# Windowed attention scores as column tiles of 32 queries: eight small matmuls of 160 keys in place of two of 256

## The chip, the cores and the metric

The kernel runs on one core of a Trainium2 chip. The metric is the device time of one execution in microseconds (us); lower is better. Several executions of the unchanged kernel are timed, and one more is taken by the hardware profiler.

## What is computed

Four sequences of 576 tokens, eight heads of 64. A query sees the 128 keys that end with its own, under a bias that falls linearly with the distance. The result feeds a mixture of four experts over all 2304 tokens, all in f32:

```python
scores = scale * np.matmul(q, k.transpose(0, 1, 3, 2))
rel = pos[:, None] - pos[None, :]
bias = slopes[:, None, None] * (-np.abs(rel).astype(np.float32))[None, :, :]
mask = (rel >= 0) & (rel < window)                      # window = 128
scores = np.where(mask, scores + bias[None], -1000000000.0)
attn = np.exp(scores - np.max(scores, axis=-1, keepdims=True))
attn = attn / (np.sum(attn, axis=-1, keepdims=True) + 1e-09)
out = np.matmul(attn, v)
...
for e in range(E):                                      # 4 experts, 512 -> 1024 -> 512
    h = np.maximum(x @ w1[e], 0.0)
    out += p[:, e:e + 1] * (h @ w2[e])
```

## The kernel before, in words

**Order.** Every piece of work is first noted as an operation of a planner (`Plan.op`): which engine may do it, a cost per engine, a due time, what it reads and writes and the buffers it needs. `Plan.order` then lays all of them out greedily, by engine, and the instructions are emitted in that order. [...] The costs are numbers in the file (`PLAIN * mm(n)` for scores, `VALUED * mm(n)` for values, and so on); an operation may also ask for a margin (`late`), which for the values operation is `LATE_V = 1.903` us. `FILL = 80` matmuls of a tile of ones into an idle bank (`multiplied`, L1827) have the latest due time of all: the planner sets one wherever it has nothing else for PE, and PE executes it there.

**Work.** The tokens are cut into seven blocks (`BLOCKS`: three of 256, four of 384) and the heads into four pairs, so there are 28 segments (block, pair). The four segments of block 0 are "plain" and done by an older recipe at the start. The other 24 segments hold 64 units, a unit being 128 queries of one pair of heads. Attention runs from the start to about 375 us, laid between the matmuls of the experts (`hidden` L1340, `output` L1760, `opening` L1248, which is the first block's first product with the expert weights; later `sevenfold` L1397 and `pair` L1656, both after or beside attention). The experts need the attention output of a block (`xh`, `xl`) before they can start on it.

**A unit** (function `unit`, not plain):

1. Scores (`scores`, L650): for each of the two heads one f32 matmul of 128 queries by up to 256 keys, the 128 of the tile before and the tile's own. Head 0 sits on partitions 0 to 63, head 1 on 64 to 127, so the two are row tiles of the array. Up to two units share one planner operation and one pair of PSUM banks.
2. Fold (L714): DVE copies, under a mask (`after`), the keys of the tile before over those own keys that the query must not see; a query then has its 128 keys in 128 columns, in rotated order.
3. DVE adds the bias and finds the maximum (L725), ACT takes exponents (L743), DVE or ACT divides (L774, L781).
4. Turn: DVE transposes blocks of 32x32 (L825), one DMA writes the unit to a DRAM buffer (`tr`), four read it back turned (`s<-tr`).
5. POOL splits it with `affine_select` into the keys of the tile itself and of the tile before (L857), into `pb`.

At a segment's last unit, values (`values`, L904) multiplies with v: 128x64 column tiles, one per head. `gathered` splits the result into `xh` and `xl`.

In the profile an f32 matmul is two records (two passes); the expert matmuls are one.

Of the kernel before, what the change touches and what calls it, by code (L numbers as in the profile page):

```python
# [16 lines left out]
NEG = -1.0e30  # L17
# [197 lines left out]
VALUED = 2.95  # L215
SWITCH = 0.09
# [67 lines left out]
def attention_moe(  # L284
# [41 lines left out]
    places("s", 3, [P, 2, 2 * P], F32)  # L326
    halves_ = [t[:, i] for t in plan.places["s"] for i in range(2)]
    plan.places["sv"], plan.places["tu"] = halves_[:NSV], halves_[NSV:]
    places("t", 6, [P, 6], F32)
    turns, again = [sb.tile([P, 6, 2 * P], F32, tag=f"pb{i}", name=f"pb{i}") for i in range(2)], {}  # L330
# [28 lines left out]
    places("tr", TURNS, [P, 2 * P], F32, dr)  # L359
# [14 lines left out]
    after = sb.tile([P, 2, P], F32, tag="after", name="after")  # L374
# [155 lines left out]
    for nb, (s0, n) in enumerate(BLOCKS):  # L530
        for hp in range(NPAIR):
            g = Rec()
            g.nb, g.hp, g.plain, g.units = nb, hp, nb == 0, []
            g.s0, g.n, g.k0 = s0, n, s0 - before(s0 // P)
            g.v0 = g.k0 // P
            g.kn, g.vn = s0 + n - g.k0, (s0 + n) // P - g.v0
            for i in range(n // P):
# [4 lines left out]
                u.q0, u.k0, u.vt = i * P, (u.tile * P - u.pk) - g.k0, u.tile - g.v0  # L542
# [70 lines left out]

    def unit(u):
# [10 lines left out]
        if g.plain:  # L625
            scored = [Buf("b"), Buf("b")]
            sh = lambda h: scored[h][:, :n]
        else:
            at = u.q0 // P
            if at % 2 == 0:  # L630
                g.scored = [Buf("b"), Buf("b")]
            scored, sc0 = g.scored, 2 * P * (at % 2)
            sh = lambda h: scored[h][:, sc0 : sc0 + n]
# [6 lines left out]
        if not g.plain:  # L640
            at = u.q0 // P
            mine = g.units[at : at + 2] if at % 2 == 0 else []

        def scores(e):
            for x in mine:
                c0 = 0 if g.plain else 2 * P * (x.q0 // P % 2)
                for h in range(2):
                    r = (lo64, hi64)[h]
                    qv, kv = (g.q, g.k) if g.plain else (g.q[:, 0], g.k[:, 0])
                    nc.tensor.matmul(  # L650
                        scored[h][:, c0 : c0 + x.pk + P],
                        qv[r, g.qo + x.q0 : g.qo + x.q0 + P],
                        kv[r, x.k0 : x.k0 + x.pk + P],
                        start=True,
                        stop=True,
                        skip_group_check=not g.plain,
                    )

        qk = [(g.shared[0], g.hp % 2, h) for h in range(2)] if g.plain else [g.q, g.k]
        if mine:  # L660
            plan.op(
                {PE: sum(PLAIN * mm(x.pk + P) for x in mine)},
# [5 lines left out]
                sum(PLAIN * mmc(x.pk + P) for x in mine),  # L668
# [6 lines left out]
        if g.plain:  # L675

# [4 lines left out]
            if pk:  # L681
                plan.op({POOL: 0.45}, seen(lambda: b2()[:, :, :P], bv, True), d - 1, [bkey], [(bb, 0)], port=(POOL,))
            else:
                plan.op({POOL: 0.45}, seen(lambda: b2()[:, :, P:], bv, False), d - 1, [bkey], [(bb, 1)], port=(POOL,))
            bv, bkey = (lambda: b2()[:, :, o:]), [(bb, 0), (bb, 1)][not pk :]
        elif edge or pk < P:
            bb = Buf("x")
            b2 = lambda: bb[:, : 2 * P].rearrange("p (h n) -> p h n", h=2)
            if edge:
                plan.op({POOL: 0.45}, lambda e: nc.gpsimd.tensor_copy(b2()[:edge], bias[:edge, hs, :]), d - 1, [bkey, "scores"], [(bb, 0)], port=(POOL,))  # L690
                plan.op({POOL: 0.2}, lambda e: nc.gpsimd.memset(b2()[edge:, :, :edge], NEG), d - 1, ["scores"], [(bb, 1)], port=())
                plan.op(
                    {POOL: 0.3},
                    seen(lambda: b2()[edge:, :, edge:], lambda: bias[edge:, hs, edge:], False),
                    d - 1,
                    [bkey, "scores"],
                    [(bb, 2)],
                    port=(POOL,),
                )
            else:  # L700
# [179 lines left out]
        if u.first:  # L880
            g.started, g.jobs = [False, False], []
            if not g.plain:
                g.av = Buf("b")
# [1147 lines left out]
```

## Time and profile before

| | |
|---|---|
| Median of 3 runs | 850.93 us (850.92 to 851.1) |
| The profiled execution's own time | 850.55 us |
| Its span, first to last instruction | 848.8 us |
| Granted TensorE clock, mean over the span | 1.00 |
| PE busy / DVE / ACT / POOL | 844.5 / 662.7 / 393.3 / 346.3 us |

Busy times count overlapping instructions once. [...]

### The profile page before, as it was taken

What the parts mean: (1) busy time and instruction counts of PE and PEld (TensorE: products, weight loads), DVE (VectorE), ACT (ScalarE), POOL (GpSimd) and SP (SyncE); (2) the same over time, 40 slices, a digit from 0 to 9 for tenths busy, and PEclk for the clock granted to TensorE, in tenths of its full rate; (3) what the DMA queues carried; (4) which work ended last, traced back from release to release, by engine and by line L of the source; (5) the groups of instructions that cost most, each with busy time, mean ns of one, the idle gap of its engine ahead of it and who ended that gap; (6) DMA issues with size and microseconds to landing.
All of it is one profiled execution on the core that took longest, in us unless ns stands there. A gap on an engine that the chain in (4) does not pass through costs nothing.

```text
span 848.8 us, 15203 instructions
## 1 busy us (share of the span) xinstructions
PE 844.5 (99%) x5050; PEld 748.3 (88%) x5050; DVE 662.7 (78%) x1621; ACT 393.3 (46%) x1019; POOL 346.3 (41%) x550
## 2 busy tenths in 40 slices
PE   9999999999999999999999999999999999999998
PEld 6888788777777778889898898998999999999998
DVE  7998767677866687748887777887798888788777
ACT  7754424354433355414553433442455544654552
POOL 2422422141332435226752326133656464454542
DMA  7877755466756467532787565744566346535602
GB/s 240 255 238 232 226 154 170 134 175 180 225 165 175 124 196 231 171 97 84 274 317 270 211 224 186 273 179 156 169 216 220 116 137 199 155 131 162 224 2 75
DMA packets 92464, 156.37 MB, mean 184 GB/s; under 512 B 42849, under 2 KB 63073, under 8 KB 88673
## 3 DMA queue, kind: packets, MB, share of 16 engines
q1 hardware_dynamic: 86528, 125.84, 45.6%
q0 software_dynamic: 5632, 29.36, 11.0%
q8 instruction: 40, 0.66, 0.3%
q14 instruction: 40, 0.32, 0.1%
q10 hardware_dynamic: 224, 0.20, 0.1%
HBM read 111.32 MB, written 44.04 MB: 183 GB/s over the span
## 4 chain that ended last, share of the span: by engine, by line
PE 98%; DVE 1%; issue 0%; ACT 0%; ACTq 0%
PE b L1760 32%; PE b L1397 25%; PE b L1340 18%; PE b L1656 13%; PE b L904 4%; PE b L650 4%; PE b L1827 1%; PE b L1248 1%; PE b L801 0%; DVE w1r L1182 0%; DVE xl L421 0%; DVE acc L725 0%; DVE b L1426 0%; DVE w1r L1570 0%; DVE q L1570 0%
## 5 line engine op out<-in xcount | busy, mean ns | idle before, releaser
L1760 PE MATMUL b<-w2h,halves 128*128 128x512 f32 x612 | 208.0, 394 | 0.0
L1340 PE MATMUL b<-xh,w 128*128 128x512 f32 (+2 forms) x576 | 153.2, 341 | 0.0
L1760 PEld LDWEIGHTS b<-w2h,halves 128*128 128x128 f32 x612 | 114.9, 188 | 26.2 <-issue 3.7
L1778 DVE SCALAR_TENSOR_TENSOR acc<-b,prob,acc 128x512 f32<-128x512 f32 x136 | 101.5, 746 | 32.3 <-PE b L1760 31.3
L1760 PE MATMUL b<-w2l,halves 128*128 128x512 f32 x306 | 120.1, 392 | 0.0
L857 POOL TENSOR_SCALAR_AFFINE_SELECT pb<-s 128x256 f32<-128x256 f32 x120 | 53.8, 473 | 153.5 <-DMA s<-tr 38.4
L1340 PEld LDWEIGHTS b<-xh,w 128*128 128x128 f32 x576 | 101.9, 189 | 13.6 <-issue 1.2
L1340 PE MATMUL b<-xl,w 128*128 128x512 f32 (+2 forms) x288 | 97.6, 339 | 0.0
L1297 ACT ACTIVATE halves<-b 128x256 fp32r<-128x256 f32 (+2 forms) x76 | 36.9, 488 | 94.4 <-PE b L1340 93.9
L421 POOL TENSOR_TENSOR w<-w1r,w 128x256 fp32r<-128x256 f32 x66 | 50.0, 779 | 73.0 <-DVE w L421 32.8
L1682 DVE SCALAR_TENSOR_TENSOR acc<-b,prob,acc 128x256 f32<-128x256 f32 x156 | 67.4, 476 | 12.2 <-PE b L1656 11.0
L1304 DVE SCALAR_TENSOR_TENSOR halves<-b,halves 128x256 fp32r<-128x256 f32 (+2 forms) x76 | 41.9, 553 | 44.6 <-ACT halves L1297 44.2
L743 ACT ACTIVATE s<-s,t 128x128 f32<-128x128 f32 x128 | 50.5, 395 | 49.8 <-DVE t L725 49.5
L1410 ACT ACTIVATE s<-b 128x384 f32<-128x384 f32 x87 | 42.6, 490 | 65.7 <-PE b L1397 65.3
L1397 PE MATMUL b<-xh,w 128*128 128x384 f32 x232 | 68.9, 337 | 0.0
L421 POOL TENSOR_TENSOR w2l<-w2r,w2h 128x256 fp32r<-128x256 f32 x52 | 39.5, 779 | 70.5 <-DVE w2l L421 23.0
L1760 PEld LDWEIGHTS b<-w2l,halves 128*128 128x128 f32 x306 | 57.5, 188 | 9.0
L401 ACT ACTIVATE w2h<-w2r 128x512 fp32r<-128x512 f32 x79 | 48.5, 625 | 24.4 <-PE b L1760 16.8
L1340 PEld LDWEIGHTS b<-xl,w 128*128 128x128 f32 x288 | 54.4, 189 | 6.1
L421 DVE TENSOR_TENSOR w2l<-w2r,w2h 128x512 fp32r<-128x512 f32 x76 | 54.9, 746 | 1.4 <-ACT w2h L401 1.2
L1397 PEld LDWEIGHTS b<-xh,w 128*128 128x128 f32 x232 | 42.9, 188 | 0.6
L1426 DVE TENSOR_TENSOR b<-b,s 128x384 f32<-128x384 f32 x58 | 32.6, 562 | 13.4 <-PE b L1397 9.1
(230 smaller groups left out, 2068.8 us busy)
## 6 DMA issues: line engine op xcount, KB each, us to landing
w2r<-in_w SPq DMA_DIRECT2D x59, 512.0 KB, 4.6
w1r<-in_w SPq DMA_DIRECT2D x43, 512.0 KB, 4.8
w<-parked POOLq DMA_DIRECT2D x16, 1024.0 KB, 5.2
parked<-w SPq DMA_DIRECT2D x13, 1024.0 KB, 4.9
tr<-s SPq DMA_DIRECT2D x64, 128.0 KB, 2.6
s<-tr SPq DMA_DIRECT2D x256, 32.0 KB, 2.5
vs<-parked POOLq DMA_DIRECT2D x8, 768.0 KB, 5.1
pt<-parked POOLq DMA_DIRECT2D x8, 768.0 KB, 4.6
```

Source lines behind the costliest of these rows:

```text
L401: return nc.scalar.activation(o(), i(), AF.Copy)
L421: by[e].tensor_tensor(out=x, in0=y, in1=f(z), op=ALU.subtract) for x, y, z in pieces(e, n, o(), a(), b())
L743: return lambda e: nc.scalar.activation(sv()[:, h, -m:], sv()[:, h, -m:], AF.Exp, bias=t[:, h : h + 1], scale=-1.0, accum_out=t[:, 2 + h : ...
L857: return lambda e: nc.gpsimd.affine_select(out=spread(2 * i + own), in_=wb.place, pattern=steps, base=0, channel_multiplier=-sign, compare ...
L1304: lambda e: nc.vector.scalar_tensor_tensor(out=lo[:, :n], in0=src(), scalar=0.0, in1=f(h[:, :n]), op0=ALU.max, op1=ALU.subtract,),
L1340: nc.tensor.matmul(bk[:, :n], a[0][:, kt, fs], b[:, kt, cols], start=kt == 0 and i == 0, stop=kt == KT - 1 and i == 2,)
L1397: nc.tensor.matmul(bank[:, :n], x(k), y(k), start=new and k == 0 and i == 0, stop=k == 1 and i == 2, skip_group_check=True,)
L1410: {ACT: act(n)}, lambda e: nc.scalar.activation(pv(p), bank[:, :n], AF.Copy), at[0] - URGENT, [bank], [p]
L1656: nc.tensor.matmul(bank[bk][part]()[:, cs], a()[:, ns], b()[:, fi, :], start=new and i != 1 and fi == 0 and j == 0, stop=fi == 1 and j == ...
L1682: nc.vector.scalar_tensor_tensor(out=ac[:, ds], in0=bank[bk][part]()[:, cs], scalar=prob[:, nt, e_ : e_ + 1], in1=ac[:, ds], op0=ALU.mult, ...
L1760: nc.tensor.matmul(bk[:, cs], a[:, ns], b[1][:, fi, cs], start=half != 1 and fi == 0 and j == 0, stop=half != 0 and fi == 1 and j == 2, sk ...
L1778: nc.vector.scalar_tensor_tensor(out=o, in0=i_, scalar=p, in1=o, op0=ALU.mult, op1=ALU.add)
```

## The change

Scores of a unit become eight matmuls: four column tiles of 32 queries (`FAST`), for each of two heads, each by the 160 keys (`WIDE`) that those 32 queries can see between them. All units of a segment, two or three, are one planner operation in one pair of banks. The order of the 128 keys left after the fold is now the same in each block of 32 queries, so the fold touches 32 columns a unit, and is done once a segment and head. The bias is rotated to match: its first 32 rows are loaded four times, and POOL makes the other heads of it; the plain segments keep the old bias in a `pb` buffer (`level`). Biases of tiles at a sequence's border are put together from more, smaller POOL pieces. A segment's weights (two or three units) go to DRAM in one write and come back in seven reads, straight into `pb`; POOL then makes the two parts with one select each for the whole segment. Units without a tile before them are no longer treated apart: they read the tile before and get a bias that hides it.

```diff
+TILED = 0.03
+SIDES = 1.1
+FAST = 32
+WIDE = 160
...
-    places("s", 3, [P, 2, 2 * P], F32)
...
+    st = sb.tile([P, 6, 2 * P], F32, tag="st", name="st")
+    plan.places["s"] = [st[:, 2 * i : 2 * i + 2] for i in range(3)]
+    plan.places["sv"], plan.places["tu"] = [st[:, i] for i in range(NSV)], [st[:, NSV:].rearrange("p i n -> p (i n)")]
...
+    def turned_over(g, wb, d, nu):
+        tr = Buf("tr")
+        m, w = 64 * nu, 2 * P * nu
+        flat_ = lambda: tr[:, :w]
+        load(lambda: flat_(), lambda: wb[:, :w], 512 * w, d + 0.8, [(wb, i) for i in range(nu)], [tr])
...
+        for kb in range(4):
+            for j0, j1 in ((0, kb + 1), (kb + 1, 4)):
+                if j0 < j1:
+                    g.rows.append((kb, j0))
+                    load(
...
+                        128 * m * (j1 - j0),
+                        d + 0.85,
+                        [tr],
+                        [(g.pt, (kb, j0))],
+                    )
...
+        plan.op({POOL: SIDES * nu / 3}, lambda e: side(e, False), d + 0.95, rows, [(g.pt, "earlier")])
+        plan.op({POOL: SIDES * nu / 3}, lambda e: side(e, True), d + 1.0, [], rows)
...
-            mine = g.units[at : at + 2] if at % 2 == 0 else []
+            mine = g.units if u.first else []
...
-                for h in range(2):
-                    r = (lo64, hi64)[h]
-                    qv, kv = (g.q, g.k) if g.plain else (g.q[:, 0], g.k[:, 0])
-                    nc.tensor.matmul(
-                        scored[h][:, c0 : c0 + x.pk + P],
-                        qv[r, g.qo + x.q0 : g.qo + x.q0 + P],
-                        kv[r, x.k0 : x.k0 + x.pk + P],
...
+                c0 = WIDE * (x.q0 // P)
+                qv, kv = (g.q[:, 0], g.k[:, 0])
+                for j in range(0, P, FAST):
+                    for h in range(2):
+                        r = (lo64, hi64)[h]
+                        nc.tensor.matmul(
+                            scored[h][j : j + FAST, c0 : c0 + WIDE],
+                            qv[r, g.qo + x.q0 + j : g.qo + x.q0 + j + FAST],
+                            kv[r, x.k0 + j : x.k0 + j + WIDE],
...
-                {PE: sum(PLAIN * mm(x.pk + P) for x in mine)},
+                {PE: sum(PLAIN * mm(x.pk + P) if g.plain else TILED + WIDE / 600 for x in mine)},
...
-        if fold and pk:
+        if fold and u.first:
+            nu = len(g.units)
             for h in range(2):
                 plan.op(
-                    {DVE: 0.07 + pk / 960},
+                    {DVE: 0.075 + nu * FAST / 960},
...
-                if pk:
-                for own in (0, 1):
-                    plan.op({POOL: 0.42}, side(own), d + 0.95 + 0.2 * own, raws_, [(g.pt, 2 * i + own)])
...
+            if u.last:
+                turned_over(g, wb, d, nu)
...
-    load(lambda: bias[:, 0, :], lambda: bfd[:, 0, :], 65536, -38, [], ["rel"], ACT)
+    level = Buf("pb")
+    load(lambda: level[:, :P], lambda: bfd[:, 0, :], 65536, -38, [], [(level, 0)], ACT)
+    for j in range(4):
+        load(lambda j=j: bias[32 * j : 32 * j + 32, 0, :], lambda: bfd[:32, 0, :], 16384, 0.1 * j, [], [("rel", j)])
...
+        plan.op({POOL: 0.8 if hp else 0.4}, rescaled(hp), 1 + hp, [("rel", j) for j in range(4)], [("bias", hp)])
```

The planner's table decides where everything lands, so three places of the order are shown. The first is on PE, in the first blocks, where a segment's scores follow the values of an earlier one (`b` is a PSUM bank, `k` and `q` the operands). Before, the pair of heads of each unit is one row each:

```order
716 L904 MATMUL b_115<-pb_85,v_67 64x128 x2
717 L904 MATMUL b_115<-pb_85,v_67 64x256 x4
718 L904 MATMUL b_115<-pb_85,v_67 64x128 x2
719 L650 MATMUL b_116<-k_66,q_64 128x256
720 L650 MATMUL b_118<-k_66,q_64 128x256
721 L650 MATMUL b_119<-k_65,q_63 128x256
722 L650 MATMUL b_121<-k_65,q_63 128x256
```

Of the changed kernel, half a unit stands here; a unit has eight such rows, one bank per head in turn, and the units of a segment follow each other without a break:

```order
158 L708 MATMUL b_113<-k_66,q_64 32x160
159 L708 MATMUL b_117<-k_66,q_64 32x160
160 L708 MATMUL b_113<-k_66,q_64 32x160
161 L708 MATMUL b_117<-k_66,q_64 32x160
```

Over the whole listing the 64 units are 128 score matmuls in 26 unbroken runs before, and 512 in 22 runs now; the values are the same rows as before.

The second place is PE's opening: `b<-xh,w` (L1248, now L1277) is the first product with expert weights, `b<-acc,v` (L904, now L933) the values of a plain segment, `b<-ident,acc` (L801, now L873) transposes of one. Before, the product begins between the plain segments:

```order
134 L904 MATMUL b_115<-acc_109,v_68 64x128
135 L1248 MATMUL b_117<-xh_89,w_97 128x256
136 L1248 MATMUL b_117<-xl_91,w_97 128x256
137 L1248 MATMUL b_117<-xh_89,w_97 128x256
138 L801 MATMUL b_118<-ident,acc_105 128x128 x2
139 L1248 MATMUL b_117<-xh_89,w_97 128x256
```

Now it begins behind the last plain segment's values, with filling matmuls on ones (L1869) ahead of them:

```order
191 L1869 LDWEIGHTS ones
192 L1869 MATMUL b_112<-ones 128x256
193 L933 MATMUL b_114<-acc_108,v_68 64x256
194 L933 MATMUL b_114<-acc_102,v_68 64x256
195 L933 MATMUL b_114<-acc_108,v_68 64x128
196 L933 MATMUL b_114<-acc_102,v_68 64x128
197 L1277 MATMUL b_119<-xh_87,w_95 128x256
```

Of the 80 fillings, 49 stand up to the opening's end before and 62 now; 18 and 14 stand later but ahead of PE's last product, 13 and 4 behind it.

The third place is SP's queue, where the weights are turned. Before, each unit has a write and four reads:

```order
101 L394 DMA tr_128<-s_78 128x256
102 L394 DMA s_78<-tr_127 32x4x64 x4
103 L394 DMA s_78<-tr_128 32x4x64 x4
104 L394 DMA tr_129<-s_77 128x256
```

Now a segment (here three units) has one write and seven reads:

```order
143 L399 DMA tr_121<-st 128x768
144 L399 DMA w2r_93<-in_w 128x1024
145 L399 DMA pb_83<-tr_121 32x192
146 L399 DMA pb_83<-tr_121 32x3x192
147 L399 DMA pb_83<-tr_121 32x2x192 x2
148 L399 DMA pb_83<-tr_121 32x3x192
149 L399 DMA pb_83<-tr_121 32x192
150 L399 DMA pb_83<-tr_121 32x4x192
```

## Rows read from the trace of the kernel before

**Rows 1.** The page: busy time by engine, and the chain that ended last.
```profile
PE 844.5 (99%) x5050; PEld 748.3 (88%) x5050; DVE 662.7 (78%) x1621; ACT 393.3 (46%) x1019; POOL 346.3 (41%) x550
...
PE 98%; DVE 1%; issue 0%; ACT 0%; ACTq 0%
```

**Rows 2.** PE's waits, all: who waited for whom, us, times, longest.
```profile
PE b L1827 <- DVE ones L1811: 1.1, 1, 1.1
PE b L650 <- DVE t L740: 0.4, 1, 0.4
PE b L650 <- DVE t L725: 0.3, 1, 0.3
```

**Rows 3.** Busy time in three stretches; count of instructions in brackets.
```profile
core 0: us, PE busy (x) PEld busy (x) DVE busy (x) ACT busy (x) POOL busy (x), PEclk, DMA share, GB/s
0.00:13.00 13.00, 11.02 (x74) 7.65 (x74) 7.12 (x40) 8.13 (x30) 3.90 (x14) 1.00 0.69 195
13.00:380.00 367.00, 367.00 (x2141) 298.01 (x2140) 272.00 (x877) 171.20 (x563) 114.05 (x229) 1.00 0.63 189
380.00:848.80 468.80, 466.45 (x2839) 442.63 (x2838) 383.60 (x706) 214.01 (x427) 228.32 (x308) 1.00 0.52 180
```

**Rows 4.** Score passes by shape: count, busy us, mean ns.
```profile
L650 PE MATMUL b<-k,q 64*128 64x256 f32 x208 | 28.7, 396 | 0.0
...
L650 PE MATMUL b<-k,q 64*128 64x192 f32 x32 | 4.3, 349 | 0.0
...
L650 PE MATMUL b<-k,q 64*128 64x128 f32 x16 | 1.7, 284 | 0.0
```

**Rows 5.** PE's timeline around four runs of score passes: start, length, count.
```profile
276.78 0.39 PE L1760 MATMUL b<-w2l,halves 128*128 128x512 f32 x1
277.00 0.39 PE L1760 MATMUL b<-w2h,halves 128*128 128x512 f32 x1
277.32 1.13 PE L650 MATMUL b<-k,q 64*128 64x256 f32 x8
278.39 0.50 PE L1760 MATMUL b<-w2h,halves 128*128 128x512 f32 x1
...
126.09 2.43 PE L650 MATMUL b<-k,q 64*128 64x256 f32 x20
128.45 1.09 PE L904 MATMUL b<-pb,v 128*64 128x128 f32 x12
129.47 0.50 PE L1760 MATMUL b<-w2h,halves 128*128 128x512 f32 x1
...
267.05 0.60 PE L650 MATMUL b<-k,q 64*128 64x192 f32 x4
267.58 0.50 PE L1340 MATMUL b<-xh,w 128*128 128x512 f32 x1
```

**Rows 6.** L650 passes begun by 67.455, 67.460, 67.775 and 67.782 us.
```profile
67.44:67.45 0.01, 0.00 (x1) 1.00 0.06 17
67.44:67.46 0.02, 0.01 (x2) 1.00 0.54 218
67.44:67.78 0.34, 0.32 (x3) 1.00 0.85 294
67.44:67.78 0.34, 0.33 (x4) 1.00 0.83 288
```

**Rows 7.** PE's timeline around a segment's values, two column tiles.
```profile
284.05 1.52 PE L904 MATMUL b<-pb,v 128*64 128x128 f32 x16
285.50 0.59 PE L650 MATMUL b<-k,q 64*128 64x192 f32 x4
```

**Rows 8.** PE's timeline in the opening, with filling matmuls.
```profile
15.76 1.69 PE L1827 MATMUL b<-ones 128*128 128x256 bf16 x14
```

**Rows 9.** SP's timeline ahead of the first expert weights.
```profile
9.36 0.43 SPq L394 DMA_DIRECT2D w1r<-in_w  x1
9.84 0.43 SPq L394 DMA_DIRECT2D w2r<-in_w  x1
10.31 0.43 SPq L394 DMA_DIRECT2D q<-in_q  x1
10.78 0.43 SPq L394 DMA_DIRECT2D w1r<-in_w  x1
```

**Rows 10.** POOL's timeline in the opening; idle time before, in brackets, and its releaser.
```profile
3.49 2.96 POOL L551 TENSOR_SCALAR_AFFINE_SELECT acc<-bias 128x256 f32<-128x256 f32 x8 [1.87 <-ACT bias L1817]
...
17.99 1.42 POOL L421 TENSOR_TENSOR w<-w1r,w 128x256 fp32r<-128x256 f32 x2 [11.54 <-ACT t L738]
```

**Rows 11.** Fold on DVE and selects on POOL: count, busy us, mean ns.
```profile
L714 DVE COPY_PREDICATED b<-after,b 128x128 f32<-128x128 uint32 x104 | 26.4, 287 | 5.3 <-PE b L650 5.1
...
L714 DVE COPY_PREDICATED b<-after,b 128x64 f32<-128x64 uint32 x16 | 3.1, 222 | 3.6 <-PE b L650 3.5
...
L857 POOL TENSOR_SCALAR_AFFINE_SELECT pb<-s 128x256 f32<-128x256 f32 x120 | 53.8, 473 | 153.5 <-DMA s<-tr 38.4 <-DVE w2l L421 26.9 <-DVE s L774 24.1
```

**Rows 12.** DMA issues of the turn: count, KB each, median us to landing.
```profile
tr<-s SPq DMA_DIRECT2D x64, 128.0 KB, 2.6
s<-tr SPq DMA_DIRECT2D x256, 32.0 KB, 2.5
```

More of the change, by code (lines that the diff above doesn't have):

```diff
@@ L373, in attention_moe @@
     plan.places["gr"] = [bias[:].rearrange("p h n -> p (h n)").rearrange("p (k n) -> p k n", k=KT)]
-    after = sb.tile([P, 2, P], F32, tag="after", name="after")
+    own = sb.tile([P, 3, FAST], F32, tag="own", name="own")
+    gone = sb.tile([P, 2, FAST], F32, tag="gone", name="gone")
     ones = sb.tile([P, P], F32, tag="ones", name="ones")
@@ L667, in unit @@
                 [] if not g.plain else [s],
-                sum(PLAIN * mmc(x.pk + P) for x in mine),
+                sum(PLAIN * mmc(x.pk + P if g.plain else WIDE) for x in mine),
                 late=late,
@@ L792, in unit @@
             g.pt = [Buf("acc"), Buf("acc")] if g.plain else Buf("pb")
-        through = not g.plain and not DIRECT >> (4 * (g.nb - 1) + g.hp) & 1
-        if not through:
+        nu = len(g.units)
+        if g.plain:
             bk2 = Buf("b")
@@ L851, in unit @@
-            raws_ = [(wb, b_) for b_ in range(4)]
-            spread = lambda slot: g.pt.place[:, slot]
-            def side(own):
-                sign = 1 if own else -1
-                steps = [[32 * sign, 4], [0, 2], [sign, 32]] if through else [[0, 2], [sign, P]]
-                return lambda e: nc.gpsimd.affine_select(
-                    out=spread(2 * i + own),
-                    in_=wb.place,
-                    pattern=steps,
-                    base=0,
-                    channel_multiplier=-sign,
-                    compare_op=ALU.is_ge if own else ALU.is_gt,
-                    fill=0.0,
-                )
@@ L892, in unit, with turned @@
         jobs, g.jobs = g.jobs, []
-        def turned(a, b, h):
-            if through:
-                return g.pt.place[:, a:b].rearrange("p s (a h c) -> p s a h c", a=4, h=2)[:, :, :, h]
-            return g.pt.place[:, a:b, P * h : P * h + P]
+        def turned(c, h):
+            at, two = c
+            x = g.pt[:]
+            ends = [[2 * P * nu + 64, 2]] if two == 2 else []
+            return bass.AP(x.tensor, x.offset + at + 32 * h, [list(x.ap[0]), *ends, [64 * nu, 4], [1, 32]])
         def values(e):
@@ L917, in unit @@
             else:
-                ps_ = [(g.pt, x) for x in range(2 * len(g.units)) if x or g.units[0].pk]
+                ps_ = [(g.pt, x) for x in ("earlier", *g.rows)]
             plan.op(
@@ L1830, in attention_moe @@
         plan.op({PE: 0.112}, multiplied, 1.0e6 + i, ["ones"], [], [idle], cold=0.214)
-    plan.op({POOL: 0.3}, lambda e: nc.gpsimd.memset(after, 1.0), -2, [], ["after"], port=())
-    plan.op(
-        {POOL: 0.45},
-        lambda e: nc.gpsimd.affine_select(
-            out=after,
-            in_=after,
-            pattern=[[0, 2], [1, P]],
-            base=0,
-            channel_multiplier=-1,
-            compare_op=ALU.is_gt,
-            fill=0.0,
-        ),
-        -2,
-        [],
-        ["after"],
+    plan.op({POOL: 0.2}, lambda e: nc.gpsimd.memset(own, 1.0), -2, [], ["own"], port=())
+    for j in range(0, P, FAST):
+        plan.op(
+            {POOL: 0.3},
+            lambda e, j=j: nc.gpsimd.affine_select(
+                out=own[j : j + FAST],
+                in_=own[j : j + FAST],
+                pattern=[[0, 3], [-1, FAST]],
+                base=0,
+                channel_multiplier=1,
+                compare_op=ALU.is_ge,
+                fill=0.0,
+            ),
+            -2,
+            [],
+            ["own"],
+        )
+    plan.op(
+        {POOL: 0.2},
+        lambda e: nc.gpsimd.tensor_scalar(out=gone, in0=own[:, :2], scalar1=1.0, scalar2=-NEG, op0=ALU.subtract, op1=ALU.mult),
+        -1,
+        ["own"],
+        ["gone"],
     )
```

195 lines of the change are left out of this document (107 added, 88 removed).

## The prediction

> **What bounds the kernel now.** I read the page first, for who is busy. PE is busy for 99% of the span and makes up 98% of the chain that ended last; DVE comes next with 78% [rows 1]. Busy time of matmuls hides waits, since records overlap, so the list of PE's waits comes second: it names three, 1.8 us in all, none of them for attention's later steps [rows 2]. Third, the stretches: from 13 to 380 us, where attention is laid between the experts' products, PE is busy in all 367.00 us, while DVE has 272, ACT 171 and POOL 114 [rows 3]. So PE's own list of work is the time. An edit gains what it takes off that list, and loses what it puts there or what it makes PE wait. Work taken from DVE, POOL or the DMA queues is worth nothing by itself.
>
> What a score matmul costs on PE is not its mean duration (396 ns, [rows 4]) but the distance between starts. A run of 8 passes (two units of 256 keys) takes 277.32 to 278.39, 1.07 us; one of 20 passes (five units) takes 126.09 to 128.45, 2.36 us [rows 5]. The difference, 1.29 us for three units, makes 0.43 us a unit, and the run itself costs 1.07 - 0.86 = 0.21 us. A unit of 192 keys: 0.53 - 0.21 = 0.32 us [rows 5]. Both are 1.7 ns a key for a unit's four passes; the 4 units of 128 keys then cost 0.22 us.
>
> The four passes of a unit run two by two. By 67.455 us one pass of a run has begun, by 67.460 the second; the third and fourth begin between 67.46 and 67.775, and by 67.782 [rows 6]. Two row tiles start some 7 ns apart, and the second rides free. Column tiles do the same: a segment's values, 16 passes, take 284.05 to 285.50, 1.45 us, or 0.09 us a pass, though half of them have 256 columns [rows 7]; at 1.7/2 ns a column they would take 0.11 and 0.22 us each, 2.6 us, one after the other.
>
> **The change, part by part.**
>
> *Scores, before.* Rows 4 hold 208, 32 and 16 passes, so 52, 8 and 4 units [rows 4]. They cost 52 x 0.43 + 8 x 0.32 + 4 x 0.22 = 25.8 us, and 26 runs x 0.21 = 5.5 us: 31.3 us.
>
> *Scores, after.* Each unit has 16 passes of 160 keys on eight tiles. No row shows more than two tiles at once, so I bound it. Below: all eight ride together, and a unit costs 160 x 1.7 = 0.27 us, 64 units 17.3 us. Above: only two ride together, as the rows show, four times 0.27 = 1.08 us, 69 us. I take 0.27: in both directions of the array the rows show the second tile free, and eight starts of 7 ns are 0.05 us, under the 0.135 us of a pass. With 22 runs x 0.21 = 4.6 us, and 0.9 us (22 x 6 more starts of 7 ns) until a run's last tile has started: 22.8 us. Gain 31.3 - 22.8 = 8.5 us. The weight loads double in number but have 32 columns in place of 128; rows do not show one of 32, I take it as hidden like the others, and if it is not, it is one of the ways to a higher price per unit.
>
> *Filling matmuls.* PE executes each where it stands, 0.109 us apart ((1.69 - 0.28) / 13, [rows 8], 0.28 being a filling's own length). Ahead of the last product 67 stood, now 76: 9 x 0.109 = 1.0 us of loss. In the opening it is 13 more, later 4 fewer. The order shows why: the first expert product now stands behind the last plain segment's values, as its operands are reckoned later.
>
> *Fold.* DVE's 120 copies take 29.5 us [rows 11]; 32 copies of 96 columns and 16 of 64, at 0.29 at most and 0.22 us, make 13. DVE loses 16 us of work. PE never waits for it outside the opening [rows 2]: nothing.
>
> *Selects.* 120 of 256 elements, 0.45 us each by busy time, become 32 of 768 and 16 of 512. By elements that is 57 us for 53.8 [rows 11]; the same, on an engine that is idle for much of the time. The border pieces and the copies add some microseconds on POOL. Nothing, as long as values do not wait.
>
> *The turn.* SP issues 64 + 256 DMAs before [rows 12], 24 + 168 now, 0.43 us each [rows 9]. But a segment's chain behind its last unit grows: write 2.6, seven issues 3.0, landing 2.5, two selects of 1.35, 10.8 us; before, 2.6 + 1.7 + 2.5 + 0.9 = 7.7 us. What hides these 3.1 us is other expert products laid ahead of the values, with 1.9 us of margin that the planner adds to its own reckoning; 24 segments over some 350 us leave 14 us for each. I take nothing. If the cover were gone, PE would stand for up to 24 x 3.1 = 74 us.
>
> *Opening.* Four bias loads stand in SP's queue ahead of the second expert weights: 4 x 0.47 us between starts, 1.9 us [rows 9]. POOL gets seven scalings of 128 elements in front of its first expert work; the nearest row is a select of 256 at 0.37 us (2.96 for 8), so 1.3 to 2.6 us. POOL had been idle for 11.54 us there [rows 10]. I take nothing beyond the fillings; with all of it on the path, 1.9 + 2.6 = 4.5 us.
>
> *Sum.* 8.5 - 1.0 = 7.5 us. On the profiled execution's own time, 850.55, that is 843.05; what lies around the span I leave as it is. The median of the runs is 0.4 us above that execution, so 843.4 us.
>
> **The rivals.**
>
> *Starts have a price of their own (no change).* If each pass on PE needs a slot, whatever its tile, 16 slots a unit can outlast the 0.27 us. The gain with its fillings is gone where a unit costs 0.27 + 7.5/64 = 0.39 us, or 24 ns a slot. The rows stand on both sides: 7 ns between two tiles [rows 6], but never more than two in a row, and 85 to 90 ns a pass as the densest stretch [rows 7]. At 24 ns 64 x 0.12 = 7.7 us come back, 851 us. [...]
>
> *Not all tiles ride together (slower).* Four of a head's column tiles read the same 64 partitions of `k` at four places; the rows show two such readers at most. If four of the eight run at once, a unit costs 0.54 us: 64 x 0.27 = 17.3 us back, 843.4 + 17.3 = 860.7 us. With two at once 64 x 0.81 = 51.8 us, 895 us. It decides from 0.39 us a unit.
>
> *The opening slips.* For it: weights later by up to 4.5 us, and 13 fillings more. Against: PE has as many score runs to do before the first product as before, and POOL was idle. 843.4 + 4.5 = 848 us at most, still faster.
>
> *Values wait for the longer turn.* From 7.5/24 = 0.31 us a segment the gain is gone; against it stands that PE does not wait for the turn once in the trace [rows 2]. A tenth of the 3.1 us exposed would make 851 us; a few segments, 1 to 4 us, 845 to 848 us.
>
> **How the numbers follow.** Forecast, all eight tiles together and PE fed: 0.60, range 840.5 to 846 (a run's own price 0.1 us lower or a unit's 0.04 higher). Opening or turn with a few us exposed, 846 to 849.2: 0.12. Slots near break-even or values exposed that far, 849.2 to 853: 0.09. Four tiles at once, about 861: 0.11. Two at once or slots far above 25 ns, beyond 870: 0.08. A run of this kernel tells 0.2%, 1.7 us, from no change. Faster by more: 0.60 + 0.12 = 0.72. Within, 849.2 to 852.6: 0.08. Slower: 0.20. Reaching from 840.5 to 853 leaves out the last two cases, 0.19.
>
> **What would show it.** In the profile after: a run of two units of score passes in about 0.79 us and of three in about 1.06 us between the first start and the next product, eight passes begun within some 50 ns, and 135 ns from one round to the next; no wait of PE for `pb` or `tr` outside the first 30 us; DVE some 16 us less busy; the first expert product (L1277) over no later than L1248 is before. The prediction is wrong if a round takes 0.2 us or more, if a row of waits for `pb` shows on PE, or if the opening ends 2 us or more later.

## The result, and the profile after

The changed kernel takes 841.3 us (median of 4 runs, 841.03 to 841.73) where the kernel before, run beside it, takes 851.01: a ratio of 0.9886, 95% interval 0.9874 to 0.9898. Forecast were 843.4 us, range 840.5 to 853. The profiled span is 839.8 us, 9.0 less than before.

The page of the changed kernel, busy time and the chain that ended last, answers to [rows 1]:

```profile
PE 834.2 (99%) x5818; PEld 742.5 (88%) x5818; DVE 654.0 (78%) x1543; ACT 392.8 (47%) x1024; POOL 358.2 (43%) x533
...
PE 96%; DVE 2%; DMA 1%; SPq 0%; issue 0%; POOL 0%; ACT 0%; DVEq 0%; POOLq 0%
```

PE has 768 matmuls more and is busy for 10.3 us less; it still is the time. Its waits, all of them, as in [rows 2]:

```profile
PE b L1869 <- DVE ones L1840: 1.1, 1, 1.1
PE b L694 <- DVE t L797: 0.5, 1, 0.5
PE b L873 <- DVE acc L846: 0.3, 1, 0.3
PE b L933 <- ACT acc L406: 0.2, 1, 0.2
```

No wait for `pb` or `tr`: the longer turn is covered. Now the runs of score passes, PE's timeline of the changed kernel (two units, then three), and after it how many L708 passes had begun by 56.20, 56.29, 56.35 and 56.43 us, as in [rows 5, 6]:

```profile
56.14 0.77 PE L708 MATMUL b<-k,q 64*32 64x160 f32 x32
56.85 0.39 PE L1369 MATMUL b<-xh,w 128*128 128x256 f32 x1
...
196.03 1.05 PE L708 MATMUL b<-k,q 64*32 64x160 f32 x48
197.00 0.50 PE L1789 MATMUL b<-w2h,halves 128*128 128x512 f32 x1
```

```profile
56.10:56.20 0.10, 0.06 (x8) 1.00 0.38 123
56.10:56.29 0.19, 0.15 (x8) 1.00 0.45 140
56.10:56.35 0.25, 0.21 (x15) 1.00 0.48 150
56.10:56.43 0.33, 0.29 (x16) 1.00 0.47 144
```

From 56.14 to 56.85 a run of two units takes 0.71 us, one of three 0.97 us. Eight passes begin at once (in the records 0, 7, 13, 20, 27, 33, 40 and 47 ns after the first), none for the next 0.1 us, then eight more: all eight tiles run together. Later rounds are 136 ns apart. The difference of the two runs is 0.27 us a unit, and a run costs 0.16 us besides. In 22 unbroken runs (8 of two units, 12 of three, 2 of six at 1.82) that is 8 x 0.705 + 12 x 0.976 + 2 x 1.816 = 21.0 us.

The stretches of the changed kernel, as in [rows 3], and the selects and predicated copies, as in [rows 11]:

```profile
13.00:380.00 367.00, 366.71 (x2970) 301.21 (x2969) 272.92 (x814) 178.21 (x578) 142.33 (x227) 1.00 0.61 190
380.00:839.80 459.80, 456.32 (x2778) 433.58 (x2776) 373.93 (x691) 206.35 (x416) 210.95 (x288) 1.00 0.53 184
```

```profile
L647 POOL TENSOR_SCALAR_AFFINE_SELECT pb<-pb 128x768 f32<-128x768 f32 x32 | 32.2, 1005 | 65.0 <-DVE w2l L426 23.6 <-DMA pb<-tr 16.3 <-PE b L1789 15.0
...
L647 POOL TENSOR_SCALAR_AFFINE_SELECT pb<-pb 128x512 f32<-128x512 f32 x16 | 12.0, 750 | 31.6 <-DVE w L426 15.4 <-DMA pb<-tr 11.7 <-DVE w L407 2.5
```

The opening is the one place that got later. POOL's and PE's timeline of the changed kernel there, as in [rows 10]:

```profile
17.96 4.72 POOL L1856 TENSOR_SCALAR bias<-bias 128x128 f32<-128x128 f32 x7 [11.51 <-DMA bias<-in_bias]
22.64 1.41 POOL L426 TENSOR_TENSOR w<-w1r,w 128x256 fp32r<-128x256 f32 x2
```

```profile
23.91 0.38 PE L1277 MATMUL b<-xh,w 128*128 128x256 f32 x1
...
30.53 0.28 PE L1277 MATMUL b<-xh,w 128*128 128x256 f32 x1
```

Before, the first and the last of those products stood here:

```profile
19.74 0.39 PE L1248 MATMUL b<-xh,w 128*128 128x256 f32 x1
...
29.37 0.28 PE L1248 MATMUL b<-xh,w 128*128 128x256 f32 x1
```

POOL begins its first weight subtraction at 22.64 us, where before it began at 17.99 [rows 10]: seven scalings of the bias stand ahead of it, and these began only when the bias had landed. The opening products begin at 23.91 and the last of them at 30.53; before, those were 19.74 and 29.37. That is 1.16 us later, from one trace each. In e_order_tile, e_order_head and e_order_two below, whose order differs only within the score passes, the last one starts at 30.05 to 30.47, so the figure is good to some 0.5 us.

**Where the 9.0 us came from.** Add up the distances from one matmul's start to the next by line, up to the last product (the records overlap: an output product's is 0.39 us long, and the next starts 0.22 us behind its start, at 277.00 for 276.78 [rows 5]). Up to the end of the opening the changed kernel is 1.16 us later. From there to the last product it is 10.31 us faster: scores 27.97 us before and 18.86 now (9.11 less), output products 0.83 less, all else 0.4 less. An output product takes some 0.1 us more (0.31 to 0.34 where 0.23 is the median) just before PE goes over to scores or values, and again just after it comes back: 32 of their distances were over 0.3 us before, 23 are now. Some of these returns went to the hidden products, which take 0.18 us more (part of the "all else"). The way from the last product's start to the end is 0.10 us longer. 1.16 - 10.31 + 0.10 = -9.05.

### The profile page after: what moved, and what is told of

Read it like the earlier page. It is cut to its first block, busy times and chain, and to the rows that moved or that the text cites. A ratio compares the mean times of both kernels' runs of the same rounds, so it can differ in the third digit from the quotient of the medians.

```text
span 839.8 us, 16374 instructions
## 1 busy us (share of the span) xinstructions
PE 834.2 (99%) x5818; PEld 742.5 (88%) x5818; DVE 654.0 (78%) x1543; ACT 392.8 (47%) x1024; POOL 358.2 (43%) x533
## 4 chain that ended last, share of the span: by engine, by line
PE 96%; DVE 2%; DMA 1%; SPq 0%; issue 0%; POOL 0%; ACT 0%; DVEq 0%; POOLq 0%
PE b L1789 32%; PE b L1426 25%; PE b L1369 18%; PE b L1685 13%; PE b L933 4%; PE b L708 2%; PE b L1277 1%; PE b L1869 1%; DMA bias<-in_bias 1%; SPq L399 0%; PE b L694 0%; DVE xl L426 0%; DVE acc L1711 0%; DVE w1r L1211 0%; DVE b L1455 0%
## 5 line engine op out<-in xcount | busy, mean ns | idle before, releaser
L1807 DVE SCALAR_TENSOR_TENSOR acc<-b,prob,acc 128x512 f32<-128x512 f32 x136 | 101.5, 747 | 34.5 <-PE b L1789 33.4
L1369 PEld LDWEIGHTS b<-xh,w 128*128 128x128 f32 x576 | 102.1, 189 | 14.5 <-issue 2.7
L426 POOL TENSOR_TENSOR w2l<-w2r,w2h 128x256 fp32r<-128x256 f32 x60 | 47.6, 815 | 100.2 <-ACT w2h L406 32.3
L647 POOL TENSOR_SCALAR_AFFINE_SELECT pb<-pb 128x768 f32<-128x768 f32 (+1 forms) x48 | 44.2, 920 | 96.6 <-DMA pb<-tr 28.0
L1439 ACT ACTIVATE st<-b 128x384 f32<-128x384 f32 x87 | 42.5, 489 | 64.1 <-PE b L1426 63.9
L406 ACT ACTIVATE w2h<-w2r 128x512 fp32r<-128x512 f32 x89 | 54.5, 626 | 27.6 <-PE b L1789 21.7
L815 ACT ACTIVATE st<-st,t 128x128 f32<-128x128 f32 x128 | 50.0, 392 | 30.6 <-DVE t L797 30.6
L426 POOL TENSOR_TENSOR w<-w1r,w 128x256 fp32r<-128x256 f32 x44 | 32.2, 752 | 46.7 <-DVE w L426 36.7
L426 DVE TENSOR_TENSOR w<-w1r,w 128x512 fp32r<-128x512 f32 x64 | 46.5, 742 | 0.1
L1455 DVE TENSOR_TENSOR b<-b,st 128x384 f32<-128x384 f32 x58 | 32.7, 563 | 13.9 <-PE b L1426 9.7
```

Source lines behind the costliest of these rows:

```text
L406: return nc.scalar.activation(o(), i(), AF.Copy)
L426: by[e].tensor_tensor(out=x, in0=y, in1=f(z), op=ALU.subtract) for x, y, z in pieces(e, n, o(), a(), b())
L647: return nc.gpsimd.affine_select(out=g.pt[:, :w] if mine else g.pt[:, w : 2 * w], in_=g.pt[:, :w], pattern=[[32 * sign, 4], [0, 2 * nu], [ ...
L815: return lambda e: nc.scalar.activation(sv()[:, h, -m:], sv()[:, h, -m:], AF.Exp, bias=t[:, h : h + 1], scale=-1.0, accum_out=t[:, 2 + h : ...
L1369: nc.tensor.matmul(bk[:, :n], a[0][:, kt, fs], b[:, kt, cols], start=kt == 0 and i == 0, stop=kt == KT - 1 and i == 2,)
L1439: {ACT: act(n)}, lambda e: nc.scalar.activation(pv(p), bank[:, :n], AF.Copy), at[0] - URGENT, [bank], [p]
```

## The experiments

All are variants of the changed kernel, each timed beside the kernel before. "Against changed" is the difference of the two ratios to before, times 851 us.

| run | what differs | median us | ratio to before (interval) | against changed |
|---|---|---|---|---|
| e_order_tile | column tile outermost in the order | 854.80 | 1.0045 (1.0029 to 1.0062) | +13.5 |
| e_order_head | head outermost | 845.77 | 0.9940 (0.9925 to 0.9955) | +4.6 |
| e_order_two | column tile outermost, two units at a time | 844.95 | 0.9932 (0.9918 to 0.9947) | +3.9 |
| e_keys5x32 | five passes of 32 keys for one of 160 | 941.48 | 1.1056 (1.1036 to 1.1075) | +99.6 |
| e_keys2x80 | two passes of 80 keys | 845.87 | 0.9943 (0.9928 to 0.9958) | +4.9 |
| e_pairs | two units to an operation | 844.23 | 0.9924 (0.9908 to 0.9941) | +3.2 |
| e_fold3 | fold done three times | 843.32 | 0.9910 (0.9895 to 0.9924) | +2.0 |
| e_turn_twice | reads of the turn issued twice | 858.26 | 1.0083 (1.0068 to 1.0098) | +16.8 |
| e_scale_dve | bias scalings on VectorE | 841.53 | 0.9892 (0.9877 to 0.9906) | +0.5 |
| e_scale_act | bias scalings on ScalarE | 841.44 | 0.9891 (0.9876 to 0.9906) | +0.4 |
| e_scale_order | scalings on POOL, but the planner lays VectorE's work beside them | 840.47 | 0.9882 (0.9866 to 0.9899) | -0.3 |
| e_fill49 | 49 fillings, not 80 | 840.98 | 0.9885 (0.9870 to 0.9899) | -0.1 |

### What makes the eight tiles run together

**e_order_tile.** The loops over units, column tiles and heads change places:

```diff
-            for x in mine:
-                for j in range(0, P, FAST):
-                    for h in range(2):
+            for x, j, h in [(x, j, h) for j in range(0, P, FAST) for x in mine for h in range(2)]:
```

> The same 16 score passes per unit, in another order: for one group of 32 queries the passes of all units of the run come first, then the next group, so that neighbours in the order meet the same two tiles again and again. Theory A (a pass waits only for the pass before it on its own tile, and passes behind a waiting one start on free tiles): a run of three units stays at 0.98 us, time 841.3. Theory B (passes start in the order written; the changed kernel was fast because its order visits all eight tiles in turn): each start waits for its tile, so a unit takes four rounds of 0.136 us where it took two; a run of three units takes 1.7 to 1.8 us, 64 units x 0.27 = 17.4 us in all, time about 858.7. B is held the likelier.

Measured: 13.5 us more, between the two theories, and the runs of passes say why: together they take 34.5 us instead of 21.0, which is all of it. Those of two units take 0.745 us, nearly as in the changed kernel (0.705), as theory A has it; those of three take 1.86 us instead of 0.98, near theory B's 1.7 to 1.8; the two of six take 3.1. PE's timeline of one run of three units, and how many of its passes had begun by 200.54, 200.81 and 200.84 us:

```profile
200.52 1.93 PE L709 MATMUL b<-k,q 64*32 64x160 f32 x48
202.38 0.50 PE L1790 MATMUL b<-w2h,halves 128*128 128x512 f32 x1
```

```profile
200.46:200.54 0.08, 0.02 (x2) 1.00 0.26 102
200.46:200.81 0.35, 0.29 (x4) 1.00 0.09 35
200.46:200.84 0.38, 0.32 (x8) 1.00 0.08 32
```

Two tiles work alone for 0.3 us, four passes in all, and only then the next two begin. In a run of two units in the same kernel the starts are 0, 6, 26, 33, 53, 60, 80 and 86 ns: all eight tiles at once, though the second unit's passes for the busy tiles stand between them in the order. So in the run of two units passes started ahead of earlier ones whose tile was busy, as theory A has it; in the run of three the next tiles began 0.3 us later, nearer theory B. In this order a tile has four passes in a row with two units (each matmul stands as two passes), and six with three.

**e_order_head.** The same edit with `for h in range(2) for x in mine for j in range(0, P, FAST)`.

> The same passes, all of one head for the whole run and then all of the other, so that neighbours visit four tiles in turn. Theory A (only the own tile's predecessor is waited for, whatever the order): 0.98 us for three units, time 841.3. Theory B (starts in the order written): four tiles at once, six rounds of 0.136 us more than... three rounds in place of none, so 0.98 + 0.41 = 1.39 us for three units, 64 x 0.136 = 8.7 us in all, time about 850.0: the whole gain of the change gone.

Measured: 4.6 us more. Two units take 0.731 us, three 1.271 (forecast for three were 0.98 by theory A and 1.39 by theory B). The second head's four tiles begin 54 ns after the first with two units, and some 322 ns after it with three, which is just behind the third pass on each of the first head's tiles (296 ns). In both orders, then, the next tiles began early (26 ns in e_order_tile, 54 here) where each busy tile had four passes ahead of them in the order, and only after some 0.3 us where each had six; five were not tried, and what sets the limit no run shows. The number of passes that wait in all does not part the cases: by the order, 12 wait here with two units when the second head starts, and only 10 in e_order_tile's run of three while the next tiles are held. Of the gain of 9.7 us nearly half hangs on an order of loops that changes no work.

**e_order_two.** The same order as in e_order_tile, two units at a time (`for i in range(0, len(mine), 2)` ahead, `x in mine[i : i + 2]`).

> The order with a group of 32 queries outermost, as in the run that lost 13.5 us, but over two units at a time and then the next two. Theory, formed on that run (one pass can wait beside the running one on each tile, and what comes behind goes on; a second one that waits for the same tile holds up all that is behind it): with two units no third pass meets a tile before the others are started, so a run of three units takes 0.98 to 1.1 us and the time is 841.3 to 844. Rival (it is the distance in the order, or that neighbours meet the same two tiles): a run of three units stays near 1.5 us or more, 851 to 855.

Measured: 3.9 us more, runs of three 1.214 us. The first two units go as in e_order_tile's run of two, again with four passes to a tile ahead of the next tiles, and 9.6 of the 13.5 us are back. But the third unit is slow: its passes start at 569, 575, 620, 704, 710, 755 ns and then some 16 ns apart, where the changed kernel starts eight within 50 ns. The expectation was out by 0.1 us a run. What holds the third unit is not settled. It begins with the run's 33rd pass, where the pace changes in the next two runs too; but so does the third unit of the changed kernel, in the same order, and that one keeps its bursts (568 to 614 ns, 703 to 750).

**e_keys5x32.** What does a start cost?

```diff
-                for j in range(0, P, FAST):
+                for c, j in [(c, j) for c in range(0, WIDE, FAST) for j in range(0, P, FAST)]:
...
-                            scored[h][j : j + FAST, c0 : c0 + WIDE],
+                            scored[h][j : j + FAST, c0 + c : c0 + c + FAST],
```

> Each score pass of 160 keys is cut into five of 32 keys; the products, the tiles and what is moved stay the same, the starts are five times as many. Theory (a start on another tile costs the 6.7 ns seen between the eight starts of a round): 40 starts x 6.7 = 0.27 us where a round took 0.136, 0.53 us per unit, 64 x 0.26 = 17 us more, about 858. Rival 1 (a start costs nearer 24 ns, and bursts of eight hide it): 40 x 24 = 0.96 us for the same columns, 64 x 1.65 = 105 us more, about 947. Rival 2 (starts cost nothing, only moved columns count): 841.3.

Measured: 99.6 us more, as rival 1 had it in sum, but not by its mechanism. PE's waits, its timeline around one run of three units (240 passes), how many of its passes had begun by 211.50 and 212.50 us, and the clock behind the stop (last column but two):

```profile
PE b L708 <- issue: 46.5, 19, 4.4
```

```profile
211.27 1.81 PE L708 MATMUL b<-k,q 64*32 64x32 f32 x191
215.06 0.76 PE L708 MATMUL b<-k,q 64*32 64x32 f32 x49 [1.98 <-issue]
215.75 0.79 PE L1789 MATMUL b<-w2h,halves 128*128 128x512 f32 x1
```

```profile
211.20:211.50 0.30, 0.23 (x32) 1.00 0.00 0
211.20:212.50 1.30, 1.23 (x147) 1.00 0.00 0
...
215.00:216.00 1.00, 0.76 (x49) 0.54 0.00 0
```

32 passes begin within 0.16 us, 5 ns apart on the mean. Then come 78 ns without a start, and then 115 in 1.0 us, 8.7 ns each, most of them in pairs with 16.6 ns from pair to pair. After 191 passes PE stops, waits for nothing that the profile shows for 1.98 us, and comes back with a granted clock of 0.54. A run of two units without such a stop takes 1.49 us, 9.3 ns a pass. So a start costs 5 ns in the first 32 and 9 ns behind them, near the theory, and 24 ns is what it comes to when the stops (46.5 of the 77 us by which the runs grew; 19 of them) and some 23 us outside the runs (at a mean granted clock of 0.966, for 0.999 in the changed kernel) are spread over the 4096 added passes.

Ahead of each stop's end the trace has a transfer. The queue that the profile calls instruction (packets, MB, share), here and in the changed kernel:

```profile
q8 instruction: 78, 1.28, 0.5%
...
q8 instruction: 46, 0.75, 0.4%
```

It carried 32 packets of 16 KB more for 4096 more passes, one for every 128. In the records of the DMA packets each of the 19 stops ends 1.1 to 1.6 us after such a packet has landed, and where a run has two or three stops they stand 128 passes apart. That PE waited there for its instructions fits these times, but is not shown: they come from one trace, and no run varies that supply by itself.

**e_keys2x80.** The same edit with 80 for `FAST` as the step and the width.

> Each score pass of 160 keys is cut into two of 80 keys. Theory, formed on the run with five passes of 32 keys (after some 32 passes that lie ready, passes come one every 8.3 ns, and only runs longer than about 120 passes stall for more): eight passes every 67 ns against the 68 ns that 80 keys take, so a round is no longer than before; runs of two units unchanged near 0.72 us, of three near 1.0 us, time 841.3 to 843. Rival (a pass has a price of about 24 ns, that run's extra time over its extra passes): 1024 more passes x 24 ns = 25 us, 866.

Measured: 4.9 us more, no stops. Two units take 0.847 us and three 1.187; all runs together 25.4 us against 21.0. Rival out, and the theory misses too: the first four rounds go nearly as forecast (they begin at 0, 93, 162 and 231 ns), and behind the 33rd pass the bursts are gone and a third unit's 32 passes take 0.34 us, 10.6 ns each, where 8.5 (68 ns over eight tiles, an estimate from the 136 ns of 160 keys) would keep the tiles busy. 4.4 us over 1024 added passes are 4.3 ns each. At 160 keys a start every 17 ns (136 over eight tiles) was enough, and the rounds of the changed kernel keep to it; at 80 keys the starts fell behind.

**e_pairs.** A price for each run of passes?

```diff
-            mine = g.units if u.first else []
+            mine = g.units[u.q0 // P : u.q0 // P + 2] if u.q0 // P % 2 == 0 else []
```

(the banks and the fold follow in twos).

> The scores of a segment are issued two units at a time (as before the change) instead of a whole segment at once; the passes themselves stay. Some 16 runs more (segments of three units become two and one), and the fold's copies one pair more for each. Theory (a run has a price of its own: 0.16 us that its length does not explain, and up to 0.3 us for coming back to products over all rows): 16 x 0.16 = 2.6 to 16 x 0.46 = 7.4 us, 843.9 to 848.7. Rival (only passes count): 841.3.

Measured: 3.2 us more, with 27 unbroken runs in place of 22 (the planner laid many singles beside others). The runs took 21.9 us, 0.9 more, 0.18 us for each added run; output and hidden products took 1.6 us more, in part because PE comes back to them from scores and values more often (28 times behind the opening, not 24). That the segment became one operation is worth some 3 us of the gain, in the orders that the planner made.

### What was held to be hidden

**e_fold3.** `[copy_predicated(...) for _ in range(3)]` for the one copy.

> Every predicated copy of the fold is done three times over instead of once (88 copies more, about 0.22 us each, some 19 us of VectorE in the middle of the chain that ends in the exponent). Theory (VectorE's time is covered; the taking away of the old fold adds was worth nothing): within 0.2% of 841.3, VectorE busy about 673 us instead of 654. Rival (the lighter VectorE is a part of the gain): 4 to 9 us slower, 845 to 850.

Measured: 2.0 us more, at the bound of what can be told. The page of this run has 21 us more of VectorE:

```profile
PE 836.3 (99%) x5818; PEld 743.2 (88%) x5818; DVE 675.3 (80%) x1639; ACT 390.9 (46%) x1024; POOL 358.6 (43%) x533
```

Matched matmul by matmul with the changed kernel, PE is 1.2 us late by the end of the opening, 0.5 more by 51 us, 0.3 more by 180 us, and loses nothing in the 660 us after. So VectorE's work is hidden nearly everywhere but in and near the opening, where a trace is good to some 0.5 us. Work taken from it may have been worth up to a microsecond there, not nothing.

**e_turn_twice.**

```diff
+                    for _ in range(2):
                     load(
```

> Each of the seven reads of a segment's turn out of DRAM is issued twice, the second behind the first: 154 reads more, and the turned weights come about 3 us later in each of 22 segments. Theory (the turn lies beside other products, and the values wait for none of it): 841 to 843, no wait of TensorE for pb. Rival (the turn has little room, by the prediction a gain was gone from 0.3 us per segment): the values wait, from 7 us (0.3 us each) up to 66 us (3 us each) more, 848 to 907.

Measured: 16.8 us more. (There are 168 added reads, since the 22 stretches of scores hold 24 segments.) PE's waits, and the windows of this run with the largest loss and of the long middle:

```profile
PE b L934 <- POOL pb L648: 2.4, 2, 2.1
PE b L1370 <- DVE xh L407: 2.0, 1, 2.0
PE b L1427 <- ACT pt L406: 1.7, 1, 1.7
PE b L1427 <- DVE pt L426: 1.2, 1, 1.2
```

```profile
80.00:110.00 30.00, 24.97 (x149) 19.08 (x148) 21.13 (x57) 11.30 (x35) 12.78 (x24) 0.94 0.68 219
140.00:400.00 260.00, 260.00 (x1992) 211.70 (x1993) 176.35 (x523) 110.30 (x371) 88.03 (x135) 1.00 0.63 194
400.00:440.00 40.00, 37.04 (x180) 33.48 (x180) 34.33 (x54) 19.69 (x37) 21.78 (x28) 0.96 0.73 260
```

From 140 to 400 us, with 14 of the 23 stretches of scores of this run, PE does not wait once. Summed over the distances between starts above the usual one of their kind, some 10 us are lost between 60 and 110 us: the values wait 2.4 us for their turned weights, the product behind them 2.0 for an operand, and the clock sags to 0.94. Another 5 are lost around 412 to 416 us, where no attention is left: there ScalarE's and VectorE's parts of a split expert operand (`pt`) come late; that this follows from the order that the planner made around the added reads is argued, not shown. So most segments hide some 3 us more of a turn, and some of those up to 110 us do not; there SP issues the second reads 0.47 us apart, as in [rows 9], and the loads behind them in its queue are late too. The theory's bound (2 us) falls, and so does the rival's picture of a loss in every segment.

### The opening

**e_scale_dve, e_scale_act, e_scale_order.** The seven scalings of L1856 on VectorE, on ScalarE, or still on POOL; in all three with `port=()`, so that the planner puts VectorE's work beside them. The third edit:

```diff
-        plan.op({POOL: 0.8 if hp else 0.4}, rescaled(hp), 1 + hp, [("rel", j) for j in range(4)], [("bias", hp)])
+        plan.op({POOL: 0.8 if hp else 0.4}, rescaled(hp), 1 + hp, [("rel", j) for j in range(4)], [("bias", hp)], port=())
```

> The seven scalings of the 128x128 bias in the opening (4.7 us of POOL from 17.96 to 22.67 us of the changed kernel's span) are done on VectorE. Theory (the opening of the changed kernel ends 1.16 us later than before because POOL is held by these scalings and the weight splits behind them come late): the first expert product comes up to 1 us earlier, fillings up to there 49 instead of 62, time 840.3 to 840.8. Rival (what is late is VectorE, which took over a cast from ScalarE): seven more instructions of about 0.2 us on VectorE make the opening later still, 842 to 843.

> The same seven scalings on ScalarE. Theory (POOL is what is late): first expert product up to 1 us earlier, fillings up to there 55 instead of 62, time 840.3 to 840.8. Rival (ScalarE is as full as POOL there): no change, 841.3.

> [...] Theory of the changed order (casts that moved from ScalarE to VectorE and behind it are what comes late): first expert product 0.5 to 1 us earlier, fillings up to there 55 instead of 62, 65 instead of 76 ahead of the last product, time about 840.5. Theory of POOL (the 4.7 us of scalings are the delay, whatever the order): 841.3.

Measured: +0.5, +0.4 and -0.3 us, none of which can be told from the changed kernel. POOL's and PE's timeline in e_scale_dve:

```profile
19.42 1.42 POOL L426 TENSOR_TENSOR w<-w1r,w 128x256 fp32r<-128x256 f32 x2 [12.96 <-DMA k<-in_k]
```

```profile
22.17 0.38 PE L1277 MATMUL b<-xh,w 128*128 128x256 f32 x1
```

Without the scalings POOL's first subtraction comes 3.2 us earlier and the opening ends 1.74 us earlier (28.91 for 30.65). That does not show that POOL was what was late there. In e_scale_act POOL is rid of the scalings too, its first subtraction stays at 22.65, and the opening ends 0.3 us earlier; in e_scale_order all seven are still ahead of it, and the opening ends 1.3 us earlier. What also moves is the first cast of the opening's weights, which was on ScalarE before. The cast before, in the changed kernel and in e_scale_order, and as the last line the scalings of e_scale_order:

```profile
17.29 0.62 ACT L401 ACTIVATE w<-w1r 128x512 fp32r<-128x512 f32 x1
...
21.36 0.94 DVE L407 CAST w<-w1r 128x512 fp32r<-128x512 f32 x2
...
19.20 0.62 ACT L406 ACTIVATE w<-w1r 128x512 fp32r<-128x512 f32 x1
...
16.84 4.32 POOL L1856 TENSOR_SCALAR bias<-bias 128x128 f32<-128x128 f32 x7 [10.38 <-DMA bias<-in_bias]
```

It begins at 18.40 us in e_scale_dve, 19.20 in e_scale_order, 21.17 in e_scale_act and 21.36 in the changed kernel, and the opening ends in the same sequence, at 28.91, 29.38, 30.32 and 30.65. So the scalings worked at least in part through the order that the planner made around them, as e_scale_order's first theory had it; what they cost on POOL alone is not separated.

Nor is the time of e_scale_dve better: from the opening's end to the last product this run takes 806.9 us, the changed kernel 805.1. Of the 1.9 us, 1.4 are fillings, 28 in place of 14, which the planner laid where it had nothing else for PE. In e_scale_order the bias lands 1.1 us earlier and nothing is given back: the span is 838.6 us for 839.8. That is the fastest version run, by less than its timing can tell.

**e_fill49.** `FILL = 49` for 80.

> Only 49 fillings instead of 80: all of them come before the end of the opening, and 27 fewer ahead of the last product. Theory of the prediction (each filling ahead of the last product costs its 0.109 us): 27 x 0.109 = 2.9 us less, 838.4. Rival (a filling lies in time in which TensorE would wait in any case, so their number only counts the waiting): 841.3, or more if the granted clock falls in the openings that they leave.

Measured: -0.1 us; the rival holds. PE's timeline in its opening:

```profile
21.28 0.66 PE L873 MATMUL b<-ident,acc 128*128 128x128 f32 x4 [0.77 <-DVE acc L846]
22.44 1.32 PE L933 MATMUL b<-acc,v 128*64 128x256 f32 x8 [0.51 <-ACT acc L406]
```

Where the fillings are gone, PE waits for the same operands, which are VectorE's and ScalarE's parts of the last plain segment and not POOL's, and the first opening product comes at 23.70 instead of 23.91. The granted clock stays 1.00.

## Why the prediction was right, step by step

- **PE's list is the time:** right. PE stays 99% busy, and what went from its list, 10.1 us of scores (9.1 of them behind the opening) and 0.8 of output products, is the gain.
- **Scores before,** 31.3 us: the distances in the trace add up to 31.1.
- **Scores after,** 22.8 us: 21.0. The 0.27 us a unit, taken from "all eight ride together", was exact. Mis-sized was the price of a run, 0.21 + 0.04 us, which is 0.16. That made the gain 10.1 for 8.5. It does hang on the order of the loops, which no step named (e_order_tile, e_order_head).
- **Fillings,** 1.0 us of loss: the count of 76 was right, the price not. PE's time in them grew by 2.0 us, from 9.5 to 11.5, but they fill waits (e_fill49): what costs there is what PE waits for.
- **Opening, "nothing beyond the fillings":** the step that failed. The seven scalings took 4.7 us, not 1.3 to 2.6, and the first subtraction had been taken to have POOL's 11.5 us of idle time ahead of it; the scalings could not use that, since they waited for the bias. With them the order changed, and the first cast of the opening's weights came at 21.36 us instead of 17.29. The opening ends 1.16 us later; which share is the scalings' own is open (e_scale_order), and what the bias loads cost by themselves no run shows. That 1.16 is nearly the 1.0 us charged for fillings is chance.
- **Fold, nothing:** nearly. VectorE lost 8.7 us (662.7 to 654.0), not 16: the planner moved subtractions for the first weights to it from POOL (64 on VectorE for 53, 44 on POOL for 66), which has the scalings and border pieces. 21 us put back cost 2.0 (e_fold3).
- **Selects:** 44.2 us for the 57 reckoned; still hidden.
- **Turn:** hidden, as taken; its room is smaller than 14 us a segment suggested, under some 3 us in some of the segments up to 110 us (e_turn_twice).
- **Not priced:** fewer returns from scores and values, 27 before and 24 now behind the opening: 0.65 us in favour, output and hidden products together.
- **The sum:** 10.1 us of scores, less 2.0 in fillings, and 1.0 elsewhere make the 9.05 of the traces, where 8.5 - 1.0 had been forecast. The mechanism was right; that the number came within 2.1 us owes something to errors on both sides.
- **Rivals.** A price of its own for each start did not come true at 160 keys: a round takes 136 ns. At 80 keys it shows with 4 ns a pass, at 32 with 100 us. The 25 ns a slot beside which the chance of 0.08 is put, no run shows as the price of a start; in its place they show 7 ns in a burst of the changed kernel, and 5 and then 9 in e_keys5x32. "Not all tiles ride together" is what the same passes do in another order: 13.5 us back, slower than before. That rival was close, and the chance of 0.11 for it was not too much.

## What to carry to other kernels

Passes on different tiles ran side by side here where each round of the order visits every tile once (eight starts in 47 ns); where busy tiles had six passes each ahead of the others, the others began only after some 0.3 us; with four each, within 54 ns. Cut the moving side only as far as a round of all tiles stays well above 8 starts of 9 to 11 ns (at 160 keys it is 136 ns; at 80, an estimated 68, the runs took 4.4 us more), and keep runs of score passes whole (each added one took 0.18 us in e_pairs). A filling in this planned order marked a wait (31 fewer changed the time by 0.1 us in e_fill49): look for the operand that is late, and see whether what is won there is given back behind it.

## What the runs showed that I had not expected

- Passes on other tiles started ahead of earlier ones whose tile was busy (0, 6, 26, 33, 53 ns in e_order_tile's runs of two units).
- 32 passes of 32 keys begin 5 ns apart on the mean, and behind them one every 9 ns; with 80 keys, one every 11. In runs of 160 passes and more PE stopped for up to 4.4 us with no wait named in the profile, and each stop ended 1.1 to 1.6 us after a packet of the instruction queue had landed; in the microsecond behind one such stop the granted clock was 0.54.
- What makes the third unit slow in e_order_two stays open; neither it nor the supply of instructions was tried by itself.
